# Clearing the ends of sixteen token lists with one indirect DMA, and entering the rare work through a conditional block

## The chip, the cores and the metric

One core of a Trainium2 chip runs the whole program. The metric is the device time of one execution in microseconds, taken as the median of several runs. The profile is one further execution with the hardware profiler on.

## The reference

The input is a causal convolution followed by a two-level mixture of experts:

```python
w = exp(weight - max(weight)); w = w / (sum(w) + 1e-9)       # 8 heads, 7 taps
x = conv(x, w)                                               # (8, 2880, 192) -> 23040 tokens of 192
g_idx = argmax(x @ w_group)                                  # one of 4 groups, weight g_w by softmax
e_idx = argmax(x @ w_expert[g_idx])                          # one of 4 experts of it, weight e_w
out[t] = g_w * e_w * (relu(x[t] @ w1[g, e]) @ w2[g, e])      # w1 192x1024, w2 1024x192
```

Each token goes to one of 16 experts, and each expert's weights act only on its own tokens.

## The kernel before, in words

**Units.** Tokens are routed in 18 units. For each unit TensorE does the convolution and the logits, VectorE picks the expert and counts, and one indirect DMA of GpSimd (L634) writes the token numbers into `idtab`, a table in DRAM that has a list for each expert. The tile `rowi` holds for each of the 128 partitions the row at which it writes; each partition writes `LH` = 32 entries, so a scatter covers 256 entries of each of the 16 lists from the list's present end on. Entries past the true end hold a value over `BIG`, which gathers and scatters ignore.

**Slots.** The rest of the program is a list of 98 slots (`plan`): 80 of 256 tokens each, in three portions of 16, 32 and 32, and 18 for the rest (the tail). For a slot GpSimd gathers the tokens (`gather`, L706) with a list of token numbers in SBUF (`idp`, or `idpt` for the tail), TensorE turns them (`turn`, L719, L720), does the first layer (`hidden`, L737) and the second (`back`, L755, L759), ScalarE and VectorE split results in a high and a low part (L742, L743) and finish a slot in `ys` (L806, L807), and GpSimd scatters `ys` to the output (L810). Expert weights come by SyncE (L655 to L657, L659) and are split by `split_one` (L671, L672, L679, L680, L686, L687). Units are interleaved with the first slots.

**What opens the third portion and the tail.** When the last unit is routed, `open_portion` reads 16 pieces of `idtab` into `idp` (L1042), each with a register of SyncE. Then `open_tail` runs piece by piece, one piece at each slot that is opened: `close_table` clears the ends of the lists, `table` works out on VectorE which expert each tail slot has, the table goes to DRAM and back (L940, L943), and 18 reads of `idtab` fill `idpt` (L1060), each with a row number loaded into a register from the table (L1018).

`close_table` must put `BIG` behind the end of each list. Before, it reads two entries of `idtab` into a tile `seen` (L824), which makes it wait for the scatters; VectorE turns them into `BIG` (L826); SyncE loads the 16 ends into registers (L828) and issues 16 writes (L832).

**Order.** A scheduler sets each engine's order at build time; within an engine, and within the queue of SyncE or GpSimd, instructions then run strictly in that order. A DMA that cannot start yet holds all that stands behind it on its queue.

**The end.** If any unit put over 256 tokens on one expert, or the tail has more than 18 slots, the table says so in `flagi`. All engines load the flag (L1160), and the rare work stands in `For_i(0, nrare, 1)` (L1210), which with this input is run zero times. In the built program a loop that is not entered goes through a block that counts up the semaphores for the body that was left out, and then jumps past the body to the loop's exit, where each engine waits for all semaphores. The last scatter of the output stands behind that exit on GpSimd.

Of the kernel before, what the change touches and what calls it, by code (L numbers as in the profile page):

```python
# [9 lines left out]
F32 = mybir.dt.float32  # L10
F32R = mybir.dt.float32r
BF16 = mybir.dt.bfloat16
I32 = mybir.dt.int32
U32 = mybir.dt.uint32
AF = mybir.ActivationFunctionType
ALU = mybir.AluOpType
AX = mybir.AxisListType
ET = mybir.EngineType

P = 128  # L20
# [3 lines left out]
SLOT = 256  # L24
PAD = -1e30
BIG = 1 << 20
NOB = 256
LH = 32
# [3 lines left out]
OOB_WHY = "the table's entries are clamped by construction"  # L32
# [3 lines left out]
def conv_moe_kernel(  # L36
# [10 lines left out]
    nc = tc.nc  # L47
# [17 lines left out]
    E = G * EG  # L65
# [14 lines left out]
    DUMMY = E * CAP  # L80
# [75 lines left out]
    const = ctx.enter_context(tc.tile_pool(name="const", bufs=1))  # L156
# [4 lines left out]
    rt = ctx.enter_context(tc.tile_pool(name="rt", bufs=2))  # L161
# [16 lines left out]
    idviews = dram_disjoint_views(idtab[:, :], NVIEW)  # L178
# [52 lines left out]
    for q, (p0, r0, n) in enumerate(((0, 0, P), (0, P, D2), (D2, P, D2))):  # L231
        c = min(q, 1)
# [13 lines left out]
    def clear_table():  # L246
# [12 lines left out]
        out=tri, in_=ones, pattern=[[1, P]], compare_op=ALU.is_gt, fill=0.0, base=0, channel_multiplier=-1,  # L259
    )  # L260

    OHE = nc.vector
    TABV = idviews[0]
    prio = const.tile([P, G], F32, name="prio")
    prioi = const.tile([P, G], I32, name="prioi")
    nc.gpsimd.iota(prioi, pattern=[[-1, G]], base=G, channel_multiplier=0)
# [3 lines left out]
    for nb in sorted({n for _, n in units}):  # L270
# [10 lines left out]
    endr = const.tile([P, E], F32, name="endr")  # L281
# [24 lines left out]
    sel = const.tile([P, E], F32, name="sel")  # L306
    nc.vector.tensor_reduce(
        out=sel, in_=ident.rearrange("p (e l) -> p e l", e=E), axis=AX.X, op=ALU.add)
    nc.gpsimd.iota(io[:, 0:1], pattern=[[0, 1]], base=0, channel_multiplier=1)
    nc.vector.tensor_scalar(  # L310
        out=io[:, 1:2], in0=io[:, 0:1], scalar1=LE - 1, scalar2=None, op0=ALU.bitwise_and)
    goff = const.tile([P, 1], F32, name="goff")
# [5 lines left out]
    for g in range(NSK):  # L318
        nc.sync.dma_start(
            out=skew[0:R, g * HG:(g + 1) * HG],  # L320
            in_=bass.AP(wvd.tensor, wvd.offset + VL - KS - (BT - 1) + g * HG * VL, [[1, R], [VL, HG], [1, VW]]),
# [13 lines left out]
    for h in range(H):  # L335
        nc.scalar.activation(
            out=band[0:R, h], in_=skew[0:R, h, BT - 1::-1], func=AF.Exp, bias=wm[0:R, h:h + 1],
# [38 lines left out]
    def unit(u, pre=None):  # L376
# [243 lines left out]
        for b0, n, ohl, ohv5 in halves:  # L620
# [13 lines left out]
        nc.gpsimd.indirect_dma_start(  # L634
            out=TABV, out_offset=bass.IndirectOffsetOnAxis(ap=rowi.bitcast(U32), axis=0),
            in_=lsi, in_offset=None,
# [179 lines left out]


    def close_table():
        ei = const.tile([1, E], I32, name="ei")
        nc.vector.tensor_copy(out=ei, in_=endr[0:1])  # L820
        yield

        seen = const.tile([P, 2, 1], I32, name="seen")
        nc.sync.dma_start(  # L824
            out=seen, in_=TABV[0:2, :].unsqueeze(0).broadcast_to([P, 2, 1]))
        nc.vector.tensor_scalar(out=seen, in0=seen, scalar1=0, scalar2=BIG, op0=ALU.bitwise_and, op1=ALU.bitwise_or)  # L826
        yield
        _, ends = nc.values_load_multi_w_load_instructions(  # L828
            ei, engines=[ET.SP], min_val=0, max_val=DUMMY - SLOT, skip_runtime_bounds_check_because=OOB_WHY,
        )  # L830
        for e in range(E):
            nc.sync.dma_start(  # L832
                out=idviews[1 + e % (len(idviews) - 1)][bass.ds(ends[e], SLOT), :].rearrange("(p r) c -> p (r c)", p=P),
                in_=seen.rearrange("p r c -> p (r c)"),
            )
            if e % 4 == 3:
                yield

    flags = const.tile([P, 2], F32, name="flags")
    flagi = const.tile([P, 2], I32, name="flagi")  # L840
# [165 lines left out]
    nrare = [None]  # L1006
# [5 lines left out]
    def open_tail():  # L1012
        yield from close_table()
        for tab[0] in table():
            yield
        idps["tail"] = const.tile([P, NTAIL, 2, 1], I32, name="idpt")
        for j in range(NTAIL):
            row = nc.values_load(  # L1018
                tab[0][0:1, j, 2:3], engines=[ET.SP], min_val=0, max_val=DUMMY,
                skip_runtime_bounds_check_because=OOB_WHY,  # L1020
            )
            tail_ids(row, idps["tail"][:, j], 2 if j < NBIG else 1)
            yield
# [97 lines left out]
    while routed[1] < portions[0][0]:  # L1121
# [5 lines left out]
        for i in [i for i, kk in enumerate(KPRE) if kk == k]:  # L1127
            e, q = divmod(i, 5)
# [78 lines left out]
        drain(tick)  # L1207


    with tc.For_i(0, nrare[0], 1):  # L1210
        nover = nc.values_load(
            flagi[0:1, 0:1], min_val=0, max_val=1, skip_runtime_bounds_check_because=OOB_WHY)
        with tc.For_i(0, nover, 1):
            for u in range(NU):
# [9 lines left out]
                    out=gi[:, 0], in0=pn, scalar1=VS.bit_length() - 1, scalar2=None, op0=ALU.logical_shift_right)  # L1224
# [4 lines left out]
                    out=ee, in0=eoff[0:BT].unsqueeze(1).broadcast_to([BT, nb, E]),  # L1229
                    in1=gb[:, 0].unsqueeze(2).broadcast_to([BT, nb, E]), op=ALU.is_equal,  # L1230
                )
                nc.vector.tensor_tensor(
                    out=ee, in0=ee, in1=eold[0:BT, u].unsqueeze(1).broadcast_to([BT, nb, E]), op=ALU.mult)
# [4 lines left out]
                    out=gr, in0=va[:, :, 1], scalar1=float(NOB), scalar2=float(BT), op0=ALU.add, op1=ALU.mult)  # L1238
                nc.vector.tensor_tensor(out=idw, in0=gr, in1=va[:, :, 0], op=ALU.add)
                for k in range(nb):  # L1240
                    nc.gpsimd.indirect_dma_start(
                        out=idtab[:, :], out_offset=bass.IndirectOffsetOnAxis(ap=gi[:, 0, k:k + 1].bitcast(U32), axis=0),
                        in_=idw[:, k:k + 1], in_offset=None,
# [48 lines left out]
```

## Time and profile before

| what | us |
|---|---|
| median of 3 runs | 1218.08 (1217.49 to 1218.64) |
| the profiled execution | 1214.05 |
| its span, first to last instruction | 1212.2 |
| TensorE busy in it | 1129.5 (93%) |
| VectorE busy | 862.2 (71%) |
| ScalarE busy | 696.7 (57%) |
| GpSimd busy | 495.0 (41%) |

The profile is read by place: a share over the whole span hides stretches in which another engine ends the wait. PE is TensorE, PEld its weight loads, DVE VectorE, ACT ScalarE, POOL GpSimd, SP SyncE; a q behind a name is the engine's sequencer or DMA queue.

### The profile page before, as it was taken

The numbers are of one execution on the slowest core, as the hardware profiler recorded it, in microseconds if no ns is written. First come the engines' busy times: TensorE is split into PE (matmuls) and PEld (weight loads), VectorE is DVE, ScalarE is ACT, GpSimd is POOL, SyncE is SP. The second block draws the span as 40 slices with busy tenths as digits, with TensorE's granted clock in tenths as the row PEclk, the third lists the DMA queues.
The fourth block names the chain that finished last, engine by engine and source line by source line (L and its number), as shares of the span: only waits on it lengthen the run. The fifth ranks groups of instructions, "written<-read, shape, count | busy, mean of one in ns | idle before, by whom it ended". The sixth has DMA issues, their size and how long they took to land.

```text
span 1212.2 us, 23621 instructions
## 1 busy us (share of the span) xinstructions
PE 1129.5 (93%) x8219; PEld 1062.1 (88%) x8219; DVE 862.2 (71%) x1835; ACT 696.7 (57%) x1362; POOL 495.0 (41%) x441
## 2 busy tenths in 40 slices
PE   5878899989899999999999999999999999999994
PEld 4444788888899999999999899999999999999994
DVE  4556998898687868676778556666666566687882
ACT  4544566665556556555644445555556555687782
POOL 2003033323334435433343434444444444577771
PEclk9989999999899999999999999999999999999997
DMA  8756588777967464543635657544444456389960
GB/s 210 215 141 153 148 223 191 204 191 195 222 192 213 118 166 137 156 119 104 162 108 145 87 137 212 153 125 137 136 129 136 129 150 162 99 247 258 263 169 15
DMA packets 169628, 195.62 MB, mean 161 GB/s; under 512 B 24932, under 2 KB 146749, under 8 KB 169502
## 3 DMA queue, kind: packets, MB, share of 16 engines
q1 hardware_dynamic: 127454, 140.43, 43.6%
q0 software_dynamic: 18720, 35.83, 10.7%
q10 hardware_dynamic: 23328, 17.80, 6.0%
q8 instruction: 65, 1.06, 0.4%
q14 instruction: 61, 0.50, 0.2%
HBM read 158.80 MB, written 36.58 MB: 161 GB/s over the span
## 4 chain that ended last, share of the span: by engine, by line
PE 66%; DVE 16%; DMA 8%; issue 4%; ACT 4%; SPq 1%; POOL 0%; POOLq 0%; DVEq 0%; ACTq 0%
PE ph L737 28%; PE po L755 17%; PE po L759 8%; PE pm L421 3%; DVE hl L743 3%; DVE ohl L599 2%; PE pm L477 2%; DMA out<-ys,idpt 2%; DMA xin<-in_x 2%; DVE cw L687 1%; DMA raw<-in_moe_w 1%; PE pm L719 1%; PE pm L720 1%; DMA xcd<-xc 1%; DVE tb L461 1%
## 5 line engine op out<-in xcount | busy, mean ns | idle before, releaser
L755 PE MATMUL po<-cw,hh 128*128 128x384 f32 x1424 | 445.8, 371 | 12.2 <-DVE ys L807 12.0
L737 PE MATMUL ph<-xa,ah 128*128 128x256 f32 x1424 | 390.0, 296 | 4.7 <-DVE hl L743 4.6
L810 POOL DMA_INDIRECT out<-ys,idp x160 | 169.2, 1058 | 474.5 <-DVE ys L807 415.4
L759 PE MATMUL po<-cw,hl 128*128 128x192 f32 x1424 | 357.8, 251 | 0.0
L743 DVE SCALAR_TENSOR_TENSOR hl<-ph,hh 128x512 fp32r<-128x512 f32 x356 | 241.2, 685 | 139.8 <-ACT hh L742 137.9
L742 ACT ACTIVATE hh<-ph 128x512 fp32r<-128x512 f32 x356 | 210.6, 593 | 204.1 <-PE ph L737 194.2
L755 PEld LDWEIGHTS po<-cw,hh 128*128 128x128 f32 x1424 | 269.7, 189 | 17.3 <-DVE ys L807 13.9
L737 PEld LDWEIGHTS ph<-xa,ah 128*128 128x128 f32 x1424 | 272.9, 192 | 7.4 <-DVE hl L743 5.0
L759 PEld LDWEIGHTS po<-cw,hl 128*128 128x128 f32 x1424 | 273.8, 192 | 2.0
L706 POOL DMA_INDIRECT xg<-xcd,idp x160 | 186.4, 1165 | 54.6 <-issue 25.9
L737 PE MATMUL ph<-xb,bh 128*128 128x256 f32 x712 | 202.8, 285 | 0.0
L737 PE MATMUL ph<-xb,bl 128*128 128x256 f32 x712 | 202.5, 284 | 0.0
L737 PE MATMUL ph<-xa,al 128*128 128x256 f32 x712 | 202.2, 284 | 0.0
L737 PEld LDWEIGHTS ph<-xa,al 128*128 128x128 f32 x712 | 137.5, 193 | 1.9
L737 PEld LDWEIGHTS ph<-xb,bl 128*128 128x128 f32 x712 | 137.7, 193 | 0.0
L737 PEld LDWEIGHTS ph<-xb,bh 128*128 128x128 f32 x712 | 137.2, 193 | 0.1
L687 DVE TENSOR_TENSOR cw<-rawc,cw 128x768 fp32r<-128x768 f32 x114 | 105.5, 954 | 16.1 <-ACT cw L686 14.0
L725 ACT ACTIVATE xb<-pm 64x256 fp32r<-64x256 f32 x98 | 36.0, 368 | 111.2 <-DVE xa L722 111.2
L672 DVE TENSOR_TENSOR al<-raw,ah 128x1024 fp32r<-128x1024 f32 x57 | 70.6, 1239 | 33.4 <-ACT ah L671 33.4
L686 ACT ACTIVATE cw<-rawc 128x768 fp32r<-128x768 f32 x114 | 90.8, 836 | 3.2 <-DMA rawc<-in_moe_w 3.2
L807 DVE SCALAR_TENSOR_TENSOR ys<-po,xg,ys 128x192 f32<-128x192 f32 x187 | 76.1, 416 | 23.1 <-ACT ys L806 16.7
L806 ACT ACTIVATE ys<-po,xg 128x192 f32<-128x192 f32 x187 | 76.1, 418 | 21.3 <-PE po L759 12.7
(258 smaller groups left out, 1601.4 us busy)
## 6 DMA issues: line engine op xcount, KB each, us to landing
rawc<-in_moe_w SPq DMA_DIRECT2D x114, 384.0 KB
raw<-in_moe_w SPq DMA_DIRECT2D x57, 512.0 KB
raw<-in_moe_w SPq DMA_DIRECT2D x114, 256.0 KB
xcd<-xc ACTq DMA_DIRECT2D x13, 1085.6 KB
xin<-in_x SPq DMA_DIRECT2D x7, 1134.0 KB
xc<-in_moe_w SPq DMA_DIRECT2D x18, 384.0 KB
xin<-in_x SPq DMA_DIRECT2D x6, 1039.5 KB
xin<-in_moe_w SPq DMA_DIRECT2D x9, 512.0 KB
```

The lines of the kernel that those rows point to most:

```text
L672: eng.get(k, nc.vector).tensor_tensor(out=al, in0=ra, in1=ah.bitcast(F32), op=ALU.subtract)
L686: pin(PINW, nc.scalar.activation(out=cw[:, fs, 0, :], in_=rc[k - 2], func=AF.Copy))
L687: eng.get(k, nc.vector).tensor_tensor(out=cw[:, fs, 1, :], in0=rc[k - 2], in1=cw[:, fs, 0, :].bitcast(F32), op=ALU.subtract,)
L706: nc.gpsimd.indirect_dma_start(out=xs[:, t, :], out_offset=None, in_=xcd[0:known, :], in_offset=bass.IndirectOffsetOnAxis(ap=ids[:, t, 0:1 ...
L737: nc.tensor.matmul(out=hp[:, j], lhsT=wgt[:, fs], rhs=xx, start=i == 0, stop=i == len(ops) - 1)
L742: nc.scalar.activation(out=hh, in_=hp, func=AF.Relu)
L743: nc.vector.scalar_tensor_tensor(out=hl, in0=hp, scalar=0.0, in1=hh.bitcast(F32), op0=ALU.max, op1=ALU.subtract,)
L755: nc.tensor.matmul(out=oo[t][:, 0:2 * D], lhsT=hh[:, j, ts], rhs=cw[:, f].rearrange("p a d -> p (a d)"), start=f == 0, stop=False,)
L759: nc.tensor.matmul(out=oo[t][:, 0:D], lhsT=hl[:, j, ts], rhs=cw[:, f, 0, :], start=False, stop=f == NF - 1,)
L806: nc.scalar.activation(out=ys[:, t, :], in_=oo[t][:, D:2 * D], func=AF.Copy, scale=g)
L807: nc.vector.scalar_tensor_tensor(out=ys[:, t, :], in0=oo[t][:, 0:D], scalar=g, in1=ys[:, t, :], op0=ALU.mult, op1=ALU.add,)
L810: nc.gpsimd.indirect_dma_start(out=outviews[nscat[0] % len(outviews)], out_offset=bass.IndirectOffsetOnAxis(ap=ids[:, t, 0:1].bitcast(U32) ...
```

## The change

A constant tile `none` filled with `BIG` is made once. `close_table` works out the rows from `endr`, the lists' ends, as a unit does for its own scatter, and writes `none` with one indirect DMA of GpSimd to the same view of `idtab` that the units use. The read of `seen`, its VectorE instruction, the 16 register loads and the 16 writes go. `close_table` has one pause in place of six, so `table` starts five opened slots earlier in the program. The rare work stands in `If(nrare != 0)`.

```diff
+    none = const.tile([P, LH], I32, name="none")
+    nc.gpsimd.memset(none, BIG)
...
     def close_table():
-        ei = const.tile([1, E], I32, name="ei")
-        nc.vector.tensor_copy(out=ei, in_=endr[0:1])
+        rows = rt.tile([P, E + 1], F32, name="rows")
+        rowi = rt.tile([P, 1], I32, name="rowi")
+        nc.vector.tensor_tensor(out=rows[:, 0:E], in0=endr, in1=sel, op=ALU.mult)
+        nc.vector.tensor_reduce(out=rows[:, E:E + 1], in_=rows[:, 0:E], axis=AX.X, op=ALU.add)
+        nc.vector.tensor_tensor(out=rowi, in0=rows[:, E:E + 1], in1=goff, op=ALU.add)
         yield
-
-        seen = const.tile([P, 2, 1], I32, name="seen")
-        nc.sync.dma_start(
-            out=seen, in_=TABV[0:2, :].unsqueeze(0).broadcast_to([P, 2, 1]))
-        nc.vector.tensor_scalar(out=seen, in0=seen, scalar1=0, scalar2=BIG, op0=ALU.bitwise_and, op1=ALU.bitwise_or)
-        yield
-        _, ends = nc.values_load_multi_w_load_instructions(
-            ei, engines=[ET.SP], min_val=0, max_val=DUMMY - SLOT, skip_runtime_bounds_check_because=OOB_WHY,
+        nc.gpsimd.indirect_dma_start(
+            out=TABV, out_offset=bass.IndirectOffsetOnAxis(ap=rowi.bitcast(U32), axis=0),
+            in_=none, in_offset=None,
         )
-        for e in range(E):
-            nc.sync.dma_start(
-                out=idviews[1 + e % (len(idviews) - 1)][bass.ds(ends[e], SLOT), :].rearrange("(p r) c -> p (r c)", p=P),
-                in_=seen.rearrange("p r c -> p (r c)"),
-            )
-            if e % 4 == 3:
-                yield
...
-    with tc.For_i(0, nrare[0], 1):
+    with tc.If(nrare[0] != 0):
```

Three places in the built order matter. The first is SyncE's queue where the third portion has been opened: the last read of `idp`, a trio of weight loads (`raw`), and the way to the tail's lists `idpt`. Before:

```order
L1042 DMA idp<-idtab 128x4
L824 DMA seen<-idtab 128x2
L656 DMA raw<-in_moe_w 64x1024
L657 DMA raw<-in_moe_w 64x1024
L655 DMA raw<-in_moe_w 128x1024
L828 TENSOR_LOAD ei
L832 REGISTER_ALU
L832 DMA idtab<-seen 128x2
...
L659 DMA rawc<-in_moe_w 128x4x192 x2
...
L943 DMA tab<-tabd 1x512
L1018 TENSOR_LOAD tab
```

Now (lines of the changed kernel; L1035 is L1042 of before, L933 is L940, L936 is L943, L1011 is L1018, L1053 is L1060, L657 to L661 are the weight loads):

```order
L1035 DMA idp<-idtab 128x4
L933 DMA tabd<-tb_ei 128x4
L658 DMA raw<-in_moe_w 64x1024
L659 DMA raw<-in_moe_w 64x1024
L657 DMA raw<-in_moe_w 128x1024
L936 DMA tab<-tabd 1x512
L1011 TENSOR_LOAD tab
L1053 REGISTER_ALU
L1053 DMA idpt<-idtab 128x2
...
L661 DMA rawc<-in_moe_w 128x4x192 x2
```

The 16 writes that stood between the trio and the read of the table are gone. The write of the table to DRAM moves from before the 16 reads of `idp` to behind them, and the next trio of weight loads, which stood behind nine of the 18 reads of `idpt`, stands behind all 18.

The second place is GpSimd at the same time, with the semaphores that each row waits for (DMAHW are landings of SyncE's and ScalarE's DMAs, DMASW of GpSimd's own). Before:

```order
L634 DMA idtab<-lsi,rowi 377088x1 [waits DMASW7_49,DVE_49]
L810 DMA out<-ys,idp_4122 23040x192 [waits DMASW0_49,DVE_49]
L706 DMA xg_206<-xcd,idp_4122 128x193 [waits DMASW1_49,Activation_49]
L810 DMA out<-ys,idp_4122 23040x192 [waits DMASW2_49,DVE_49]
L706 DMA xg_206<-xcd,idp_4122 128x193 [waits DMASW3_49,Activation_49]
L810 DMA out<-ys,idp_4122 23040x192 [waits DMASW4_49,DVE_49]
```

Now:

```order
L636 DMA idtab<-lsi,rowi 377088x1 [waits DMASW7_49,DVE_49]
L812 DMA out<-ys,idp_4124 23040x192 [waits DMASW0_49,DVE_49]
L708 DMA xg_208<-xcd,idp_4124 128x193 [waits DMASW1_49,Activation_49]
L812 DMA out<-ys,idp_4124 23040x192 [waits DMASW2_49,DVE_49]
L708 DMA xg_208<-xcd,idp_4124 128x193 [waits DMASW3_49,Activation_49]
L827 DMA idtab<-none,rowi 377088x1 [waits DMAHW3_49,DMAHW4_49,DMAHW2_49,DMAHW5_49,DMAHW1_49,DMAHW6_49,DMAHW0_49,DMAHW7_49,DMASW7_49,DMASW4_49]
L812 DMA out<-ys,idp_4124 23040x192 [waits DMASW5_49,DVE_49]
```

The new scatter waits for the landing of the reads of `idp`, and the slot's output scatters and gathers stand behind it.

The third place is GpSimd at the end. Before, a loop that is not entered takes the first pair of ISA and branch, and jumps to the row with the long wait behind the body:

```order
L1160 TENSOR_LOAD flagi
L1210 COMPARE_AND_BRANCH
L1210 ISA
L1210 UNCONDITIONAL_BRANCH
...
L1210 REGISTER_ALU
L1210 COMPARE_AND_BRANCH
L1210 UNCONDITIONAL_BRANCH
L810 DMA out<-ys,idpt 23040x192
```

Now the pair for the block that is not entered stands behind the body, next to the last scatter of the output:

```order
L1153 TENSOR_LOAD flagi
L1203 COMPARE_AND_BRANCH
L1204 TENSOR_LOAD flagi
...
L1243 UNCONDITIONAL_BRANCH
L1203 ISA
L1203 UNCONDITIONAL_BRANCH
L812 DMA out<-ys,idpt 23040x192
```

The exit with its waits for all semaphores is gone from this path on each engine; SyncE has such waits once, behind its own part of the end. The jump across the body moves from behind the ISA to the compare.

## Rows read from the trace of the kernel before

**Rows 1.** The page: the chain that ended last, shares by engine.

```profile
PE 66%; DVE 16%; DMA 8%; issue 4%; ACT 4%; SPq 1%; POOL 0%; POOLq 0%; DVEq 0%; ACTq 0%
```

**Rows 2.** Busy by stretch: us; PE, PEld, DVE, ACT, POOL (instructions); granted clock; DMA share, GB/s.

```profile
680.00:690.00 10.00, 10.00 (x71) 10.00 (x70) 5.75 (x10) 4.36 (x10) 5.13 (x5) 0.87 0.65 43
690.00:700.00 10.00, 10.00 (x80) 10.00 (x79) 7.07 (x11) 6.81 (x12) 4.16 (x5) 1.00 0.70 120
```

**Rows 3.** Line L719, two turns each, by stretches 665:690, 690:710, 712:730; first and last start.

```profile
L719 PE MATMUL pm<-ident,xg x4: 270/271/272, 671.0 to 685.8; 128*128 128x128 f32 x4
L719 PE MATMUL pm<-ident,xg x4: 270/272/274, 695.4 to 705.4; 128*128 128x128 f32 x4
L719 PE MATMUL pm<-ident,xg x4: 271/272/273, 715.0 to 728.0; 128*128 128x128 f32 x4
```

**Rows 4.** The chain that ended last, from 655 to 680: start, us, what.

```profile
662.25 3.47 DMA idtab<-lsi,rowi
...
665.94 0.36 SPq L1042
...
673.47 0.33 SPq L1042
...
673.85 2.99 DMA seen<-idtab
```

**Rows 5.** VectorE in order of time, 669 to 681: start, us, what, [idle before <-releaser].

```profile
670.26 0.68 DVE L743 SCALAR_TENSOR_TENSOR hl<-ph,hh 128x512 fp32r<-128x512 f32 x1
676.87 0.17 DVE L826 TENSOR_SCALAR seen<-seen 128x2 int32<-128x2 int32 x1 [5.92 <-DMA seen<-idtab]
```

**Rows 6.** TensorE in order of time, 671 to 680: its one wait.

```profile
679.34 0.69 PE L755 MATMUL po<-cw,hh 128*128 128x384 f32 x1 [3.03 <-DVE ys L807]
```

**Rows 7.** The chain from 705 to 730, and ScalarE in order of time there.

```profile
712.73 4.67 DMA raw<-in_moe_w
...
717.76 1.06 ACT L679 ACTIVATE bh<-raw 128x1024 fp32r<-128x1024 f32 x1 [5.96 <-DMA raw<-in_moe_w]
```

**Rows 8.** Issues of SyncE by line: L832 in 670 to 700, L1060 in 704 to 712.

```profile
L832 SPq DMA_DIRECT2D idtab<-seen x16: 332/332/376, 677.5 to 694.7; - x16
...
L1060 SPq DMA_DIRECT2D idpt<-idtab x9: 333/333/381, 705.0 to 711.7; - x9
```

**Rows 9.** GpSimd in order of time, 660 to 700.

```profile
662.25 1.00 POOL L634 DMA_INDIRECT idtab<-lsi,rowi  x1 [2.09 <-DVE pos L865]
...
671.53 1.03 POOL L706 DMA_INDIRECT xg<-xcd,idp  x1 [0.30 <-issue]
...
689.08 1.01 POOL L810 DMA_INDIRECT out<-ys,idp  x1 [3.95 <-DVE ys L807]
```

**Rows 10.** GpSimd's queue, line L1210, 1194 to 1196 and 1196 to 1199.5.

```profile
L1210 POOLq COMPARE_BRANCH  x1: 45/45/45, 1194.2 to 1194.2; - x1
...
L1210 POOLq EVENT_SEMAPHORE  x4: 17/43/43, 1196.7 to 1197.0; - x4
L1210 POOLq INC_SWDGE_SEM  x1: 1822/1822/1822, 1197.1 to 1197.1; - x1
```

**Rows 11.** The chain that ended last, 1176 to 1213, its last part.

```profile
1198.95 2.53 issue
1201.48 0.04 POOLq L1210
...
1202.68 0.04 POOLq L810
...
1203.26 1.19 POOLq L1288
```

**Rows 12.** GpSimd's last scatter in order of time, and its drains at the end (L1288).

```profile
1203.48 0.97 POOL L810 DMA_INDIRECT out<-ys,idpt  x1 [8.03 <-issue]
...
L1288 POOLq DRAIN  x3: 46/109/8052, 1203.3 to 1211.9; - x3
```

**Rows 13.** GpSimd in order of time near the start.

```profile
12.11 0.23 POOL L309 IOTA lts<- 128x1 int32 x1 [4.54 <-DVE ebase L280]
```

## The prediction

> **What bounds the kernel now.** I read the page first, then the engines' busy time by stretch, then the waits of the stretches that fell out. TensorE holds 66% of the chain that ended last [rows 1], and where nothing disturbs it there is a slot each 9.8 us: its turns start at 695.4 and 705.2 (the second start of that slot, 0.2 before the 705.4 shown), and a stretch of 10 us holds 80 of its instructions [rows 2, 3]. It is then at its own pace, and a microsecond lost there is lost to the end. So the change is worth what it takes out of TensorE's gaps, plus what it takes off the end behind TensorE's last work. Three places count.
>
> *Gap A, 676 to 690.* The slot turned at 671.0 is followed by one at 685.6 (685.8 less 0.2): 14.5 us against 9.8, so 4.75 us too many [rows 3]. VectorE stood 5.92 us before L826, for the DMA into `seen` [rows 5]. In order behind it stood the work that frees TensorE's `po` (L743, L722, L726, L807), so TensorE ran dry for 3.03 us, until L807 had come [rows 6]. The other 1.7 us are the granted clock: it is at 0.87 in 680 to 690, right after the idle time, so part of that stretch ran at the lower of its two levels (1.2 against 2.4 GHz), and it holds 71 instructions where the next holds 80; nine are 1.1 us [rows 2]. The chain shows why `seen` is late: the last unit's scatter lands at 665.7 (662.25 + 3.47), then SyncE issues 16 reads of `idp`, 665.94 to 673.8, and only then reads `seen`, which takes 2.99 [rows 4].
>
> *Gap B, 711 to 723.* Turns at 715.0 and 727.8: 12.8, so 3.0 too many [rows 3]. ScalarE waited 5.96 for weights, which had been issued at 712.7 and took 4.67 [rows 7]. They were issued that late because SyncE's queue first did the 16 writes of L832, 677.5 to 694.7, and nine reads of `idpt`, up to 711.7 [rows 8].
>
> *The end.* GpSimd reaches the loop's compare at 1194.2, waits to 1196.7 for the landing of scatters, counts the semaphores up with one instruction of 1.82, and jumps at 1198.9 [rows 10]. From the jump to the exit's first instruction is 2.53, the exit's twelve waits take to 1202.5, the last scatter starts at 1203.48, and a drain of 8.05 on GpSimd's queue ends the span [rows 11, 12].
>
> **The change part by part.**
>
> *`seen` and its VectorE instruction go.* VectorE no longer waits at 670.95. Its next instruction needs ScalarE's part of a result already under way, so it follows at once and gap A closes: I take all of 4.75. If the clock fell for another reason than the 3.03 us of idling, only 3.03 come back; if VectorE found another wait there, nothing.
>
> *The three new VectorE instructions* have the size of L826, 0.17 each, and start before 650, in place of a cast of the same size; the scheduler moves two small instructions of `table` behind the next `hl` in exchange. Net nothing, at most 0.3 against gap A's neighbour.
>
> *`none`'s memset* stands ahead of GpSimd's iotas near the start, and GpSimd then idles 4.54 us for VectorE [rows 13]: hidden. Without that cover it would cost about 0.2.
>
> *The new scatter* has the form of L634: 1.0 us on GpSimd, 3.47 from start to landing [rows 4, 9]. It waits for the landing of the 16 reads. The last is issued at 673.47; by the 2.99 of `seen` it lands at 676.5. GpSimd is free at 672.6 (the gather at 671.53), so it is held about 4 us and free again at 677.5. Behind it stand the slot's two output scatters and two gathers. Without gap A the first of them would be ready at about 674.5 (a slot's scatter starts 3.5 after its turn, 689.08 against 685.6), so all four come 3 us late. Who waits? GpSimd idles 3.95 before the next slot's scatter [rows 9], which takes the delay up, and gathers are made more than a slot ahead: the one of 671.53 was used at 685.8. I take nothing; what is late beyond about 8 us would stop TensorE's turn one for one. Where the queue's wait ends late by 1 us more, nothing changes.
>
> *SyncE's 16 writes, 16 register loads and the read of the ends go.* The queue then runs: table to DRAM at 673.9, trio of weights by 676, table back once it has landed (by twice the 2.99, 679.8), and reads of `idpt` when the new scatter has landed, 676.5 + 3.47 = 680.0, so from about 680.5 in place of 705.0. Nine reads took 6.7 us, 0.84 each [rows 8]; 18 take 15.1, and two weight DMAs between them about 1. So the next trio of weights, though now behind all 18 reads, is issued at about 697 in place of 712.2, and lands by 702. ScalarE could have used it at 711.8 (717.76 - 5.96), which is 707.0 with gap A closed: 5 us to spare, and gap B closes. I take all of 3.0; the other bound is 0, if the queue is 5 us later than this sum plus the 3.0 that the gap may grow back.
>
> *The loop becomes an If.* The counting block stays, with its 1.82. The exit's twelve waits go from GpSimd's path (1.05), and so does the jump of 2.53 behind the count. It does not vanish: the block for "not entered" now stands behind the body, so the compare at 1194.2 makes the long jump. It would arrive at 1196.8, when the landing for which it must wait anyhow has come (1196.7). Then six small waits of 0.09, the count of 1.82, a branch as at 1202.5 (0.15), one more small wait, and 0.80 to the scatter: 1196.8 + 0.5 + 1.8 + 0.15 + 0.1 + 0.8 = 1200.1 in place of 1203.48. I take 3.35. If the jump is not covered, 0.8 is left; if the drain's end does not follow the scatter, 0.
>
> The Trainium skill states (Runtime: NRT & Kernel Launch, "Instruction fetch mechanics") that a taken branch to a page which is not in the window forces a fetch before execution goes on. The 2.53 us of rows 11 agree with that. By the rule alone the If saves no fetch at all, and the end would gain only its twelve waits.
>
> *Sum:* 4.75 + 3.0 + 3.35 = 11.1 us. On the profiled execution's own terms that is a span of 1201.1 and a time of 1214.05 - 11.1 = 1203.0. The runs' median is 4.0 above the profiled execution, and I take the same sum from it: 1218.08 - 11.1 = **1207.0**.
>
> **The rivals.**
>
> *One gap stays, the end is shortened.* For it: the trio that closes gap B stands behind more reads than before, and the new scatter puts a landing ahead of them. Against: 5 us to spare. With B left, 1218.08 - 8.1 = 1210.0; with A left and B gone, 1211.7.
>
> *The end gives nothing, or only its waits.* For it: the drain of 8.05 is far longer than the scatter, and nothing shows what it waits for; and by the skill's rule the fetch stays. Against: the jump falls into a wait of 2.5 us. Both gaps alone: 1218.08 - 7.75 = 1210.3; with the waits' 0.8, 1209.5.
>
> *The change does not do what it says:* the time stands, since the landing for which `seen` waited is only waited for elsewhere, and TensorE's gaps with it. For it: the new scatter waits for later landings than `seen` did. Against: now it is GpSimd that waits, and GpSimd idles there. About 1217.
>
> *Slower.* The place is the new scatter in GpSimd's queue. If the reads' or its own landing is late by X, the reads of `idpt` and the trio behind them are late by X as well, and TensorE waits for weights. It keeps gap B from closing at X = 5, eats B's 3.0 at 8, and all of 11.1 at about 16; slower by 0.2% from 18.5 on. Such a landing would be six times the 3.47 shown. At X = 20: 1222.
>
> **How the numbers follow.** Likeliest, both gaps and the end: 0.62. The end gives little: 0.16. One gap stays: 0.11. No change: 0.06. Slower: 0.05. The likeliest case's own bounds are 1205.0 (the small DMAs that go give something back too, and the median moves by 1 us) to 1209.0. The range reaches to the cases with one gap or without the end, 1204.0 to 1212.0, and leaves out the last two. A measurement of this kernel tells 0.2%, 2.4 us, from no change. Faster: 0.88, the first three cases less 0.01. Same: 0.07. Slower: 0.05.
>
> **What would show it.** In the changed kernel's profile VectorE has no wait near 671, TensorE's turns from 671 to 730 come each 9.8 us, and the granted clock is 1.00 from 680 to 690. ScalarE does not wait for `raw` at 707. GpSimd's new scatter starts near 676.5, after idling 4 us; the reads of `idpt` begin near 680.5. At the end, GpSimd's gap of 2.5 lies between the compare and the first wait, and the last scatter starts some 6 us after the compare in place of 9.3; the drain is still 8 long. The prediction is wrong if a gap of TensorE stands in 670 to 720 for a landing, or if the drain ends at the same distance from the compare as now.

## The result and the profile after

The changed kernel takes 1204.4 us in the median of six runs (1200.28 to 1207.65), the kernel before 1216.9 in six runs beside it: a ratio of 0.9898 (95% interval 0.9871 to 0.9925), or 12.5 us less. A second set of runs gave 0.9895 (0.9852 to 0.9937). The forecast was 1207.0, in a range from 1204.0 to 1212.0.

The profiled execution took 1207.65 with a span of 1205.9. It is the longest of its six, because its start is late: the first slot is turned at 131.1 us against 123.0 before. In the fourteen profiles taken for this study that first turn stands anywhere from 122.5 to 134.7, and the two earliest of them belong to kernels with the new clearing of the lists. In this execution TensorE waited 3.58 us, until 26.7, for a load of `x` (TensorE in order of time; in brackets the idle time and what ended it):

```profile
26.70 1.32 PE L423 MATMUL ph<-xin,band 126*120 126x288 f32 x2 [3.58 <-DMA xin<-in_x]
```

So two executions are compared from a common point on. I take four: the turn of the slot behind the last unit (660.4 before, 666.0 after), the turn of the first tail slot, the last turn, and the end of the span. Between the first two lie all the slots that gaps A and B are in ("middle"), then the tail, then the end.

| kernel | middle | tail | end | turn behind the last unit |
|---|---|---|---|---|
| before | 390.3 | 130.0 | 31.5 | 660.4 |
| after | 382.5 | 129.5 | 28.0 | 666.0 |
| after, second profile | 382.5 | 130.6 | 28.0 | 660.5 |

The middle gives 7.8 us and the end 3.5. From the turn behind the last unit to the end the second profile has 541.1 us where the first has 539.9; at most 1 us of difference had been expected, and all of it lies in the tail. Line L721 of after is L719 of before; these turns answer to [rows 3], by stretches 665:690, 690:712 and 712:730:

```profile
L721 PE MATMUL pm<-ident,xg x6: 270/272/273, 666.0 to 687.1; 128*128 128x128 f32 x6
...
L721 PE MATMUL pm<-ident,xg x4: 271/273/273, 696.6 to 706.6; 128*128 128x128 f32 x4
...
L721 PE MATMUL pm<-ident,xg x4: 271/272/273, 716.2 to 726.2; 128*128 128x128 f32 x4
```

Each first start is one slot behind the one before it: 686.9 (687.1 less 0.2), 696.6, 706.4, 716.2, 726.0, 9.8 us apart. The slots of 14.5 and 12.8 us are gone. This execution reaches the place of gap A 5.6 us later, at 682 to 696. Busy time by stretch (columns as in [rows 2]) shows the granted clock at 1.00, and 80 instructions of TensorE in 680 to 690 where 71 were:

```profile
680.00:690.00 10.00, 10.00 (x80) 10.00 (x79) 6.18 (x11) 5.46 (x11) 5.21 (x5) 1.00 0.68 148
690.00:700.00 10.00, 10.00 (x80) 10.00 (x80) 6.64 (x12) 6.00 (x12) 4.08 (x4) 1.00 0.46 120
```

VectorE in order of time: behind the `hl` after which [rows 5] had 5.92 us of idle time (9.9 us behind the turn there, 10.3 here) the next `hl` now follows after 0.97, and that wait is for ScalarE:

```profile
676.28 0.69 DVE L745 SCALAR_TENSOR_TENSOR hl<-ph,hh 128x512 fp32r<-128x512 f32 x1
677.93 0.69 DVE L745 SCALAR_TENSOR_TENSOR hl<-ph,hh 128x512 fp32r<-128x512 f32 x1 [0.97 <-ACT hh L744]
```

GpSimd in order of time, for [rows 9]: the new scatter starts 15.9 us behind the turn (681.87 less 666.0), the slot's own scatters and gathers right behind it. By the profile the landing that it waited for last was the write of the table (`tabd`), which now stands behind the 16 reads:

```profile
677.55 1.03 POOL L708 DMA_INDIRECT xg<-xcd,idp  x1 [0.30 <-issue]
681.87 1.14 POOL L827 DMA_INDIRECT idtab<-none,rowi  x1 [3.29 <-DMA tabd<-tb_ei]
683.31 0.98 POOL L812 DMA_INDIRECT out<-ys,idp  x1 [0.30 <-DVE cw L689]
```

SyncE's queue in order of time, for [rows 8]: table, weights, table back, 18 reads of `idpt`, and the next trio of weights at 704.76, which is 38.8 behind the turn where it was 51.8 (712.2 less 660.4):

```profile
682.05 0.30 SPq L936 DMA_DIRECT2D tab<-tabd  x1
688.09 2.85 SPq L1053 DMA_DIRECT2D idpt<-idtab  x4
691.06 0.94 SPq L661 DMA_DIRECT2D rawc<-in_moe_w  x2
692.87 11.79 SPq L1053 DMA_DIRECT2D idpt<-idtab  x14
704.76 0.50 SPq L658 DMA_DIRECT2D raw<-in_moe_w  x1
```

ScalarE in order of time, where [rows 7] had 5.96 us of waiting for these weights:

```profile
711.48 1.06 ACT L673 ACTIVATE ah<-raw 128x1024 fp32r<-128x1024 f32 x1 [0.30 <-PE ph L739]
```

And the end, for [rows 10 to 12]. GpSimd's queue at the If (L1203), and its drains (L1281), by line:

```profile
L1203 POOLq EVENT_SEMAPHORE  x6: 17/30/43, 1193.9 to 1194.3; - x6
L1203 POOLq COMPARE_BRANCH  x1: 53/53/53, 1191.3 to 1191.3; - x1
L1203 POOLq INC_SWDGE_SEM  x1: 1855/1855/1855, 1194.4 to 1194.4; - x1
...
L1281 POOLq DRAIN  x3: 46/109/8135, 1196.9 to 1205.6; - x3
```

GpSimd's last scatter, in order of time:

```profile
1197.14 0.97 POOL L812 DMA_INDIRECT out<-ys,idpt  x1 [4.55 <-DVEq L1203]
```

From the compare to the last scatter are 5.9 us (1197.14 less 1191.3) in place of 9.3. A gap of 2.6 now lies between the compare and the first wait, 1191.3 to 1193.9, where one of 2.53 stood behind the count [rows 11].

### The profile page after: what moved, and what is told of

Read it like the earlier page. It is cut to its first block, busy times and chain, and to the rows that moved or that the text cites. A ratio compares the mean times of both kernels' runs of the same rounds, so it can differ in the third digit from the quotient of the medians.

```text
span 1205.9 us, 23515 instructions
## 1 busy us (share of the span) xinstructions
PE 1128.5 (94%) x8219; PEld 1062.2 (88%) x8219; DVE 862.2 (71%) x1836; ACT 699.3 (58%) x1362; POOL 494.2 (41%) x443
## 4 chain that ended last, share of the span: by engine, by line
PE 68%; DVE 16%; DMA 8%; ACT 4%; issue 3%; POOL 0%; SPq 0%; POOLq 0%; ACTq 0%; DVEq 0%
PE ph L739 28%; PE po L757 18%; PE po L761 8%; PE pm L423 3%; DMA xg<-xcd,idpt 3%; DVE hl L745 2%; DVE ohl L601 2%; DMA xin<-in_x 2%; PE pm L479 2%; DVE cw L689 1%; PE pm L722 1%; PE pm L721 1%; DMA rawc<-in_moe_w 1%; DVE tb L463 1%; DVE bl L682 1%
## 5 line engine op out<-in xcount | busy, mean ns | idle before, releaser
L757 PEld LDWEIGHTS po<-cw,hh 128*128 128x128 f32 x1424 | 269.5, 189 | 13.5 <-DVE ys L809 10.2
L809 DVE SCALAR_TENSOR_TENSOR ys<-po,xg,ys 128x192 f32<-128x192 f32 x187 | 76.4, 416 | 23.3 <-ACT ys L808 15.6
```

Source lines behind the costliest of these rows:

```text
L757: nc.tensor.matmul(out=oo[t][:, 0:2 * D], lhsT=hh[:, j, ts], rhs=cw[:, f].rearrange("p a d -> p (a d)"), start=f == 0, stop=False,)
L809: nc.vector.scalar_tensor_tensor(out=ys[:, t, :], in0=oo[t][:, 0:D], scalar=g, in1=ys[:, t, :], op0=ALU.mult, op1=ALU.add,)
```

## Experiments

Twelve kernels ran; the second profile of after above is one of them. All ratios are to the kernel before. Lines are those of each kernel.

### The lists alone, and the If alone

The changed kernel with `For_i(0, nrare[0], 1)` again, and the kernel before with `If(nrare[0] != 0)`.

> The lists' ends are cleared by the one indirect DMA, but the rare work stands in the counted loop as before. Theory of the prediction: gaps A (4.75 us) and B (3.0) close, the end stays, so about 7.75 us less than the kernel before (1209, ratio 0.9936); in the profile GpSimd's compare stands about 9.3 us ahead of the last scatter, and no wait of TensorE in 671 to 730. Rival, the end gave nothing and the lists gave all that the changed kernel gained: 12.5 us less (1204.4, ratio 0.990). Rival, the changed kernel's gain lies mostly in the end: 0 to 3 us less.

> The rare work stands in the If, the lists' ends are cleared by sixteen writes as before. Theory of the prediction: 3.35 us less than before (1213.5, ratio 0.9972), compare to last scatter 5.9 us in place of 9.3, gaps A and B as before. Rival, the end's drain does not follow the scatter: no difference. Rival, only the twelve waits are saved: 0.8 to 1.05 us less.

The lists alone: 0.9915 (0.9892 to 0.9939), 1205.0 us. The If alone: 0.9972 (0.9947 to 0.9997), 3.4 us less. In the stretches:

| kernel | middle | tail | end |
|---|---|---|---|
| lists alone | 382.5 | 129.8 | 31.8 |
| If alone | 392.3 | 131.7 | 27.9 |

The lists act in the middle and the If at the end: the end with the lists alone is that of a loop, and with the If alone that of after. The middle of the If alone has the lists of before and yet takes 392.3 us where before took 390.3. Its slots in the places of gaps A and B are 15.9 and 13.4 us long in place of 14.5 and 12.8 (line L719 by stretches 665:690 and 709:729, first and last start; the second start of a slot is 0.2 behind its first):

```profile
L719 PE MATMUL pm<-ident,xg x4: 270/272/273, 668.8 to 684.9; 128*128 128x128 f32 x4
...
L719 PE MATMUL pm<-ident,xg x4: 270/272/273, 714.0 to 727.6; 128*128 128x128 f32 x4
```

So the gaps themselves differ by 2 us between two profiles of the same code, and the lists are worth 7.8 us against one profile and 9.8 against the other. The interval of the lists alone (7.4 to 13.1 us on 1216.3) holds both; the forecast 7.75 is near its low end. GpSimd's last scatters with the lists alone, in order of time, and then with the If alone:

```profile
1184.52 0.97 POOL L812 DMA_INDIRECT out<-ys,idpt  x1 [0.30 <-DVE hl L786]
1193.90 0.97 POOL L812 DMA_INDIRECT out<-ys,idpt  x1 [8.40 <-issue]
```

```profile
1195.85 0.97 POOL L810 DMA_INDIRECT out<-ys,idpt  x1 [0.30 <-DVE hl L784]
1201.36 0.97 POOL L810 DMA_INDIRECT out<-ys,idpt  x1 [4.53 <-DVEq L1210]
```

### One gap at a time

The first kernel takes VectorE's wait away and keeps SyncE's sixteen writes; the second keeps VectorE's wait and takes the writes away. The first is the kernel before with one line changed:

```diff
-        nc.vector.tensor_scalar(out=seen, in0=seen, scalar1=0, scalar2=BIG, op0=ALU.bitwise_and, op1=ALU.bitwise_or)
+        nc.gpsimd.tensor_scalar(out=seen, in0=seen, scalar1=0, scalar2=BIG, op0=ALU.mult, op1=ALU.add)
```

The second is the kernel with the lists alone and these lines ahead of its indirect DMA (the `yield` is one more pause of `close_table`):

```diff
+        seen = const.tile([P, 2, 1], I32, name="seen")
+        nc.sync.dma_start(
+            out=seen, in_=TABV[0:2, :].unsqueeze(0).broadcast_to([P, 2, 1]))
+        nc.vector.tensor_scalar(
+            out=none[:, 0:2], in0=seen.rearrange("p r c -> p (r c)"), scalar1=0, scalar2=BIG,
+            op0=ALU.bitwise_and, op1=ALU.bitwise_or)
+        yield
```

> Of the kernel before only one thing is changed: the read entries are turned into the fill value by GpSimd and not by VectorE, so VectorE has no wait for them; the sixteen writes of SyncE and the counted loop stay. Theory 1, as the prediction's sum has it, gaps A and B are worth 4.75 and 3.0 each for itself: 4.75 us less (1212.1, ratio 0.9961), with a gap B of 3 us left. Theory 2, the weights of gap B are issued when SyncE's queue gets to them, at a time that TensorE's gap A does not move: gap A closes and gap B grows from 3.0 to about 7.75, no difference in time (1216.9).

> The one indirect DMA clears the ends, but its first two columns of fill are still made by VectorE from entries that SyncE reads back, so VectorE's wait of before is back; the counted loop is kept. Theory of the prediction: gap A stays with its 4.75 us, gap B closes: 3.0 us less than before (1213.9, ratio 0.9975). Rival, the two gaps have one cause, VectorE's wait: nothing gained.

Without VectorE's wait but with the writes: 0.9988 (0.9965 to 1.0011), nothing gained; the middle took 392.5. Gap A is closed (turns at 673.2 and 683.0), but the slot turned at 692.7 took 16.2 us, the one after it, where gap B stood, 11.0, and one turned at 739.6 took 12.1. In the first of these ScalarE waited for weights of another kind, `rawc`, and TensorE behind it (in order of time):

```profile
704.18 0.84 ACT L686 ACTIVATE cw<-rawc 128x768 fp32r<-128x768 f32 x1 [6.23 <-DMA rawc<-in_moe_w]
...
706.67 0.58 PE L737 MATMUL ph<-xa,ah 128*128 128x256 f32 x1 [4.05 <-DVE hl L743]
```

Issues of SyncE by line show where it stood: `rawc` (L659) is issued among the writes (L832), of which one held the queue for 3.09 us, and it is used 11 us after its issue. Before, it was issued 29.1 us behind the turn and first used 38.2 behind it, with no wait; here it was issued 30.2 behind the turn, and ScalarE, with gap A closed, was ready for it at 35.4. In the other two ScalarE waited 2.29 and 5.27 us for trios of `raw`. In the slot of 16.2 us TensorE also waited 0.96 us for a gather of GpSimd, which now stood 4.33 us for `seen`.

```profile
L659 SPq DMA_DIRECT2D rawc<-in_moe_w x2: 396/422/449, 692.7 to 693.2; - x2
...
L832 SPq DMA_DIRECT2D idtab<-seen x16: 332/332/3094, 679.7 to 697.1; - x16
```

Busy time by stretch shows the DMA engines nearly full while the writes run, 0.97 busy for 108 GB/s, where after has 0.68 for 148 in the stretch of the same name:

```profile
680.00:690.00 10.00, 10.00 (x80) 10.00 (x79) 4.83 (x9) 5.26 (x10) 6.88 (x7) 1.00 0.97 108
```

But by queue (packets, MB, share of the 16 engines) it is not the small writes that fill them. SyncE's queue, q1, with the writes and the weights, took 25.8%; the queue of GpSimd's gathers and scatters, q0, took 68.4%, and in after it took 13.5% for nearly as many packets. The stretch 680 to 690, first without VectorE's wait, then in after:

```profile
q0 software_dynamic: 237, 0.51, 68.4%
q1 hardware_dynamic: 1517, 0.54, 25.8%
```

```profile
q1 hardware_dynamic: 768, 1.06, 53.7%
q0 software_dynamic: 224, 0.41, 13.5%
```

GpSimd's transfers were thus long on the engines beside the writes. That the writes are the reason, and that `rawc` was late by this and not by its place in the queue alone, is not shown.

So theory 2 is right that gap A by itself is worth nothing, but not in its place: most of the time came back as a wait for `rawc`, ahead of the trio of gap B.

With VectorE's wait but without the writes: 0.9981 (0.996 to 1.0003), 2.3 us less by the ratio, with no change still inside the interval. The middle took 389.0: 1.3 us less than before, 3.3 less than with the If alone. Gap B is closed; the slot of gap A is 15.4 us long, between the 14.5 and 15.9 of those two. VectorE's wait is back (in order of time):

```profile
673.68 0.17 DVE L830 TENSOR_SCALAR none<-seen 128x2 int32<-128x2 int32 x1 [5.80 <-DMA seen<-idtab]
```

Against the two middles with the lists of before, 390.3 and 392.3, the two parts are worth 7.8 to 9.8 together; alone VectorE's wait is worth -2.2 to -0.2 and the writes 1.3 to 3.3.

### How much can be late

The indirect DMA three times and four times in a row (`for _ in range(3):` and `range(4):` ahead of it).

> The changed kernel, with its one indirect DMA for the lists' ends issued three times in a row, the same data to the same rows; each waits for the landing of the one before. By a scatter's 3.47 us to landing the list's reads and the weights behind them are some 5 to 7 us later than in the changed kernel. Theory of the prediction, 5 us to spare: 0 to 2 us slower than the changed kernel (1204 to 1206.5). Rival, nothing to spare: in the changed kernel ScalarE began with these weights 0.25 us after they had landed, so all but what TensorE has in hand is lost: 4 to 7 us slower (1208.5 to 1211.5), with a wait of ScalarE for raw.

> As the kernel with three, but four in a row: the reads and the weights are 8.5 to 10.5 us later than in the changed kernel. Theory of the prediction: 3.5 to 5.5 us slower than the changed kernel (1208 to 1210). Rival, nothing to spare: 8 to 10.5 us slower (1212.5 to 1215), which is nearly the time of the kernel before. By either theory the step from three to four is 3.5 us, one landing.

Three: 0.9956 (0.9933 to 0.9979). Four: 0.9945 (0.9921 to 0.997). The intervals cover each other, so the step from three to four is not told by the times. The middles are 389.6 and 390.6 against 382.5, so 7.1 and 8.1 us are lost. The rows show that neither theory had the place. TensorE waits for a gather, not ScalarE for weights. With three, GpSimd in order of time, and behind it TensorE:

```profile
686.50 1.77 POOL L828 DMA_INDIRECT idtab<-none,rowi  x1 [3.54 <-DMA tabd<-tb_ei]
692.47 0.98 POOL L828 DMA_INDIRECT idtab<-none,rowi  x1 [4.21 <-DMA idtab<-none,rowi]
694.93 0.97 POOL L828 DMA_INDIRECT idtab<-none,rowi  x1 [1.48 <-DMA idtab<-none,rowi]
696.21 0.99 POOL L812 DMA_INDIRECT out<-ys,idp  x1 [0.30 <-issue]
```

```profile
705.85 0.33 PE L721 MATMUL pm<-ident,xg 128*128 128x128 f32 x1 [4.13 <-DMA xg<-xcd,idp]
```

The turn behind the last unit is at 670.4 here, so the pairs behind the scatters start 25.8 after it, 8.5 later than in after (683.31 less 666.0 is 17.3). The two slots at the late gather are 6.3 us longer than two of after, of which 4.1 is this wait and the granted clock of 0.83 in 700 to 710 accounts for most of the rest. With four scatters the pairs are 10.6 later (695.77 less 667.8, from the same view) and the two slots 7.4 longer. What is lost beyond this, 0.8 us in both, is spread over the other slots, which take 9.80 us here and 9.77 in after. The first scatter also took longer than the 3.47 of the sum: the second starts 5.97 behind it, the third only 2.46 behind the second. With four it is 5.91, then 2.47 and 2.42. No run says why the first is the longer.

Then the weights alone were to be made late, by reading the table back twice and three times on SyncE's queue:

```diff
-        nc.sync.dma_start(out=tabt, in_=tabd.unsqueeze(0))
+        for _ in range(2):
+            nc.sync.dma_start(out=tabt, in_=tabd.unsqueeze(0))
```

> The changed kernel, with the read of the tail's table from DRAM issued twice, the second behind the landing of the first: SyncE's reads of idpt and the weights behind them come some 5 us later, GpSimd is not held. Theory of the prediction, 5 us to spare for the weights: no difference from the changed kernel up to 1 us. Rival, nothing to spare (ScalarE began 0.25 us after their landing in the changed kernel): ScalarE waits up to 5 us for raw, and TensorE loses 3 to 5 us (1207.5 to 1209.5).

> The same read three times: the weights behind it come some 10 us later. Theory of the prediction: 5 us slower than the changed kernel, with a wait of ScalarE for raw near 716 (as in gap B of before). Rival, nothing to spare: 8 to 10 us slower, about the kernel before without its gap A. Should the first doses of the repeated scatter have lost their time by these weights and not by the late gathers, the loss here is as large as there.

Twice: 0.9884 (0.9841 to 0.9928), middle 382.5. Three times: 0.988 (0.984 to 0.9921), middle 382.5. Nothing is lost, but the dose was not given. The repeats were quick, and the trio is issued 37.0 and 37.6 us behind the turn (710.4 less 673.4, 700.7 less 663.1), no later than the 38.8 of after. Issues of SyncE by line, with two and with three reads:

```profile
L937 SPq DMA_DIRECT2D tab<-tabd x2: 231/266/301, 689.0 to 694.3; - x2
...
L658 SPq DMA_DIRECT2D raw<-in_moe_w x1: 223/223/223, 710.4 to 710.4; - x1
```

```profile
L937 SPq DMA_DIRECT2D tab<-tabd x3: 215/232/296, 679.0 to 686.2; - x3
...
L658 SPq DMA_DIRECT2D raw<-in_moe_w x1: 1000/1000/1000, 700.7 to 700.7; - x1
```

These two say nothing on how late the weights may be, and serve as two more profiles of the changed kernel. The nearest other evidence is a kernel below whose lists are those of after: there ScalarE waited 0.30 us for the trio, 45.6 behind its turn of 667.1, and the slot was of the usual 9.8.

```profile
712.68 1.06 ACT L673 ACTIVATE ah<-raw 128x1024 fp32r<-128x1024 f32 x1 [0.30 <-DMA raw<-in_moe_w]
```

### The end

Three kernels. In the first, the changed kernel, the flag is made late, from `lasty`, the last slot's `ys`, so that the compare stands behind the last scatter:

```diff
-        if i == len(plan) - 6:
-            nrare[0] = nc.values_load(
-                flagi[0:1, 1:2], min_val=0, max_val=1, skip_runtime_bounds_check_because=OOB_WHY)
...
+    flagj = const.tile([P, 2], I32, name="flagj")
+    nc.vector.scalar_tensor_tensor(
+        out=flagj, in0=lasty[0][:, 0, 0:2], scalar=0.0, in1=flags, op0=ALU.mult, op1=ALU.add)
+    nrare[0] = nc.values_load(
+        flagj[0:1, 1:2], min_val=0, max_val=1, skip_runtime_bounds_check_because=OOB_WHY)
     with tc.If(nrare[0] != 0):
```

The second is the kernel with the lists alone, without the first part of the loop's body:

```diff
     with tc.For_i(0, nrare[0], 1):
-        nover = nc.values_load(...)
-        with tc.For_i(0, nover, 1):
...
```

The third is the changed kernel without the whole block:

```diff
-    with tc.If(nrare[0] != 0):
...
```

> The changed kernel, but the flag for the rare work is made by VectorE from a value that depends on the last slot's result, so that GpSimd issues the last scatter ahead of the compare and not behind the count. The scatter starts at about 3.4 us earlier than now, the compare at about 3.5 us later. Theory 1, the drain of 8 us ends a fixed time behind the last scatter (7.9 us from its start in both kernels): 3 us faster than the changed kernel (1201). Theory 2, the drain takes its 8 us from the moment at which GpSimd's queue reaches it, whatever came before: the queue reaches it about 3 us later, so 3 us slower than the changed kernel (1207).

> The lists as in the changed kernel, the counted loop as before, but the rare work in it is cut to its last part (the sorting anew of all tokens is left out, which this input never enters), so that GpSimd's jump past the body passes some twenty instructions in place of over two hundred. Theory of the prediction, the 2.53 us behind the jump is a fetch of far code: with the short way it is under 0.5 us, and the last scatter stands some 2 us nearer to the compare than in the kernel with the lists alone (7 in place of 9.3 us); 2 us faster than that kernel. Rival, a jump that is taken costs 2.5 us however near its target: the rows and the time of the kernel with the lists alone.

> The changed kernel without the rare work and its block (which this input does not enter): no compare, no count, no jump. The last scatter can follow the last result at once, 3.3 us earlier than in the changed kernel. If the drain of 8 us starts when GpSimd's queue reaches it, the end comes 3.3 us earlier (ratio to the changed kernel 0.9973). If something else holds the end, no difference.

| kernel | ratio (interval) | end |
|---|---|---|
| after, two profiles | 0.9898 (0.9871 to 0.9925), 0.9895 (0.9852 to 0.9937) | 28.0, 28.0 |
| compare behind the last scatter | 0.9906 (0.9868 to 0.9943) | 29.8 |
| loop, short body | 0.9877 (0.9844 to 0.991) | 26.8 |
| no rare work | 0.9901 (0.9866 to 0.9936) | 24.7 |

The times can't part these four, since their intervals cover each other; the end by the profile can: over the profiles that share it, it is 27.9 to 28.3 with the If of after (seven) and 31.5 to 31.8 with the loop of before (four). With the compare behind the scatter, GpSimd's last scatter in order of time:

```profile
1194.45 0.97 POOL L813 DMA_INDIRECT out<-ys,idpt  x1 [1.25 <-DVE flagj L1203]
```

and its drains by line (L1285):

```profile
L1285 POOLq DRAIN  x3: 46/103/6930, 1200.5 to 1208.0; - x3
```

The drain begins 6.0 us behind the scatter's start and still takes 6.93. So theory 2 is right: it is paid from where GpSimd's queue reaches it, nearly whole. The end is 1.8 longer, less than the 3 expected, because the drain is 1.2 shorter.

With the short body, GpSimd's queue at the loop in the stretches 1189 to 1192.5 and 1192.5 to 1196:

```profile
L1203 POOLq COMPARE_BRANCH  x2: 38/42/45, 1190.0 to 1192.3; - x2
...
L1203 POOLq EVENT_SEMAPHORE  x12: 42/43/43, 1192.6 to 1193.6; - x12
```

The same with the lists alone, 1188 to 1193:

```profile
L1203 POOLq EVENT_SEMAPHORE  x12: 43/43/43, 1191.9 to 1192.8; - x12
L1203 POOLq COMPARE_BRANCH  x2: 38/40/41, 1189.0 to 1192.9; - x2
```

From the second branch, 1192.25, to the exit's first wait are 0.4 us where the long body has 2.9 with the lists alone and 2.53 before [rows 11]. The end is 5.0 shorter than with the lists alone: 2.5 of it are the jump, and 2.5 the wait for the landing of scatters ahead of the count, which this shorter body does not have; the count begins 0.3 behind the compare, not 2.9. The ends of 31.8 and 26.8 show it; a time 2 us shorter than with the lists alone is within what the two ratios allow, not told by them. By the Trainium skill (Runtime: NRT & Kernel Launch, "Instruction fetch mechanics") a taken branch whose target is outside the window forces a fetch before execution goes on. This run agrees: the near jump takes 0.4 us, the far one 2.5 to 2.9.

Without the block the last scatter comes as soon as the last result is there (GpSimd in order of time), and the end is 24.7.

```profile
1198.08 0.97 POOL L812 DMA_INDIRECT out<-ys,idpt  x1 [1.25 <-DVE ys L809]
```

So by the end of the profile what the If still costs is 3.3 us. The times don't show it: 1208.55 us without the block and 1205.63 for the changed kernel beside it, where 3.3 less had been expected. This profile's tail is 132.4 us, the longest of the fourteen, with TensorE waiting for single gathers as in other profiles; whether that is chance or comes with the block's absence is open. The 3.3 isn't to be had without losing the rare work in any case.

## Why the prediction was right

**The sum.** 4.75 + 3.0 + 3.35 = 11.1 was forecast. The middle gave 7.8 and the end 3.5, together 11.3. The timed difference of 12.5 has an interval of 9.1 to 15.7. What is left over is within what moves from execution to execution: the start by 12 us, the tail by 3, and the gaps of before by 2. Of the 2.6 us between the forecast 1207.0 and the measured 1204.4 the six runs of before account for 1.2 (1216.9 in place of 1218.1). That the sum meets the profiles to 0.2 us is in part luck: against the longer gaps of the If alone the middle gave 9.8, and the measured 1204.4 lies below the likeliest case's own bound of 1205.0.

**Gap A: right in size.** The slot of 14.54 is one of 9.82, so 4.7 came back, with the clock. In the If alone the same slot was one of 15.9, so 6.1 would have. Against it stands the neighbour, the slot behind the last unit: 11.1 in place of 10.7, with TensorE 1.07 us idle for L809 (in order of time) where it was 0.62 for L807.

```profile
672.28 0.44 PE L757 MATMUL po<-cw,hh 128*128 128x384 f32 x1 [1.07 <-DVE ys L809]
```

I had allowed 0.3 for `table`'s instructions that moved there; 0.4 is what it came to.

**Gap B: right in size.** 12.79 became 9.76, 3.0. No run separates the removal of the sixteen writes from the earlier start of `table`, which has fewer pauses ahead of it; both bring the trio forward in SyncE's queue, from 51.8 to 38.8 us behind the turn.

**That the two can be priced one by one: wrong.** The rival "one gap stays" was put at 1210.0, as if A's 4.75 could be had with B's cause in place. The kernel that does this gained nothing: TensorE, freed earlier, met weights issued among the sixteen writes that were not there yet. With the writes gone and VectorE's wait kept, gap A stays and gap B's 3.0 is within the 1.3 to 3.3 that this gave. So the writes must go for either gap's time to come back, and VectorE's wait as well for gap A's. The sum came out because the change did both.

**The new scatter: right in time, too generous in what it allows.** It was forecast at 16.1 behind the turn (676.5 less 660.4) and came at 15.9, with 3.29 us of idle time for about 4. TensorE has no wait that comes from it. But "5 us to spare" for the weights was mis-sized: the table took 5.2 us to come back (issued at 682.05, loaded into a register at 687.23), not 2.99, so the reads of `idpt` begin 22.1 behind the turn in place of 20.1, and the trio is issued at 38.8, not 36.6. ScalarE's first use of it came 45.5 behind the turn, and in the kernel without the rare work, at 45.6, it waited for the landing: little or nothing was to spare. And the slower rival, whose place was the weights, had the wrong place: when the scatter was made late, the gathers behind it on GpSimd bound first, and 10.6 us too late cost the whole gain of the middle, for which that rival's terms ask some 12.8 (5 to spare and 7.75).

**The end: right, by the steps it named.** Compare to scatter was forecast at about 6 and is 5.9; the jump is covered by the landing (the scatter ahead of it starts at 1191.62, the waits begin at 1193.9 and none is long; before, the wait for such a landing was over 2.25 us behind the scatter's start); the drain is 8.1 long again. One reason was wrong: I spoke of a drain that follows the scatter. It follows the point where the queue reaches it. Both moved by the same amount here, so the sum did not show it.

**The memset of `none`: hidden,** as forecast. It takes 0.21 us from 6.08 on, and the instruction of [rows 13] idles less before it and starts no later (GpSimd in order of time):

```profile
12.03 0.23 POOL L311 IOTA lts<- 128x1 int32 x1 [4.39 <-DVE ebase L282]
```

## What to carry to other kernels

When a wait is taken out of a busy stretch, look for the next late thing on the queue that the same work loads, and price the two together; a gap's length is what it costs to the end only if nothing else is waiting behind it. Many small DMAs cost their issue on the queue (here sixteen, with two weight loads among them, took 17 us of SyncE's) and make late whatever is queued among and behind them; look also at how long other queues' transfers take beside them. At a program's end, a branch over code that is not run is worth placing so that its jump lies beside a wait that must be made anyhow. Shortening the code that is jumped over took 2.5 us off the jump; the two together were not tried.

## What the runs showed of the hardware that was not expected

- GpSimd's drain at the end takes 8.05 to 8.15 us where it stands right at the last scatter, and still 6.93 where that scatter started 6.0 us earlier. It is not a wait for the scatter alone.
- A jump over some two hundred instructions took 2.5 and 2.9 us on GpSimd in two kernels, over some twenty 0.4.
- The first of three indirect writes to the same rows held the next for 5.97 us, the second for 2.46; of four 5.91, 2.47 and 2.42.
- While sixteen writes of 1 KB ran, the DMA engines were 0.97 busy at 108 GB/s, most of it GpSimd's transfers (68.4% where after has 13.5), and a weight load issued among them was used 11 us later.
- In the middle stretch the undisturbed slots average 9.772 us after and 9.787 before. Over some 36 slots this is 0.5 us, what the gaps and their neighbour (4.7 - 0.4 + 3.0) leave over of the middle's 7.8. It doesn't come of the change: before and the If alone agree to 0.001, and so do the two profiles of after, but the kernel with the compare behind the last scatter, which has the lists of after, takes 9.797. No run says why.
- The first turn stood at 122.5 to 134.7 us whatever the kernel. This spread at the start, not the change, sets how well a time of this kernel can be told from another.
